# Sine matrices from the sine table instead of from the cosine matrices, and the output bias and row sums moved to other places on TensorE

## The chip, the cores and the metric

The kernel runs on one core of one Trainium2 chip. A core has five engines that run side by side and wait for each other through semaphores: TensorE (PE in the profile; PEld is its weight load), VectorE (DVE), ScalarE (ACT), GpSimd (POOL) and SyncE (SP), which here only starts transfers. Each engine works through its own list of instructions in order: an instruction that waits holds up everything behind it on that engine. The metric is the device time of one execution in microseconds (us). Before the change it is 1546.71 us, the median of three runs that lie between 1543.02 and 1546.88 us.

## The reference, cut to what matters

The program is a forward and backward pass of one block with two mixers: a spectral filter A and a two-layer perceptron B, each behind a modulated layer norm.

```python
def _A_ref(x, w_r, w_i):                      # spectral mixer
    X = jnp.fft.rfft2(x.astype(jnp.float32), axes=(-2, -1))
    X = X * (w_r + 1j * w_i)
    return jnp.fft.irfft2(X, s=(S, D), axes=(-2, -1)).astype(jnp.bfloat16)

def _B_ref(x, w1, b1, w2, b2):                # perceptron, F = 3584
    y = _layernorm(x, axis=-1)
    h = _gelu(jnp.einsum('bsd,df->bsf', y, w1) + b1)
    return jnp.einsum('bsf,fd->bsd', h, w2) + b2

sa, ca, ga, sb, cb, gb = (mod[:, k] for k in range(6))   # mod = silu(c) @ w_mod
h = _layernorm(x) * (1 + ca) + sa
x = x + ga * _A_ref(h, A_w_r, A_w_i)
h = _layernorm(x) * (1 + cb) + sb
x = x + gb * _B_ref(h, B_w1, B_b1, B_w2, B_b2)           # this is out
# reference(): out and the gradients of x, w_r, w_i, w1, b1, w2, b2, c, w_mod for grad_out
```

x is 2048 tokens by 1024 features. The gradient of gb is a sum over the tokens of grad_out times B's output; that output is needed with its bias b2.

## The kernel before: the parts that the change touches

The Fourier transforms are matrix products with cosine and sine matrices, which the kernel makes itself at its start. An index is worked out on GpSimd (`pts`, line 353), reduced modulo the period on VectorE (line 380), and sent through the Sin function of ScalarE (line 381). `gidx` has two halves that are used in turn. Only the cosine matrices CE and CO are made in this way; the sine matrices SE and SO come out of them by `turn`, a GpSimd multiplication of the reversed matrix by a sign for each partition.

```python
genv = reg.tile([P, 3136 + 3 * P], BF16, name="genv", tag="px2")   # index vectors, small rows for b1 and b2
...
def turn(dst, mat):
    pts(dst, mat, sgn[:], None, ALU.mult)                          # GpSimd

def trig(dst, colv, rowv, nrow, width, modn):
    idx = gidx[:, gcount[0] % 2, :]
    gcount[0] += 1
    sh = float(3 * modn // 4)
    for r in range(nrow):
        pts(idx[:, r*width:(r+1)*width], colv, rowv[:, r:r+1], sh, ALU.mult, ALU.add)      # GpSimd, L353
    n = nrow * width
    nc.vector.tensor_scalar(out=idx[:, 0:n], in0=idx[:, 0:n], scalar1=modn - 1, ..., op0=ALU.bitwise_and)  # L380
    nc.scalar.activation(out=dst, in_=..., func=ACT.Sin, bias=negpi[:], scale=2 * np.pi / modn)            # L381
...
# gen_mats: see the diff.  After it, on GpSimd:
nc.gpsimd.dma_start(out=out_7..., in_=gb2r)                        # gradient of b2, L649; gb2r lies in genv
```

The tile `ws2` of the spectral stage has the tag px2 as well, so its loads on SP's queue (L479) can only start when everything that reads `genv` is done. Behind them on the same queue stand the loads of `wt` (L281), transposed pieces of w2 for the first matrix product of the perceptron's gradient (`ph_part`, `pp`, L669). `ph_part` is spread over the spectral stage, to keep TensorE at work while VectorE folds, unfolds and normalizes.

```python
def load_w2t(fg):                                                  # L281, two buffers
    nc.sync.dma_start_transpose(out=wt[:, fg % 2], in_=B_w2[fg * 256:(fg + 1) * 256, :])
for fc in range(PH_EARLY):                                         # PH_EARLY = 6
    ph_part(fc, (0, 1, 2, 3))                                      # 32 matmuls each
    if fc % 2 == 1:
        load_w2t(fc // 2 + 2)
```

The perceptron's forward pass runs in four blocks of 512 tokens. `z_block` (32 matmuls `pz`, then the gelu and its derivative) alternates with seven pieces of `bo_pass` (16 matmuls `pbo` each), once for each block b and half h of the features. TensorE's order is fixed in this stage by `ordered()`.

```python
def bo_pass(b, h):
    pbs = [(ps_f if b < NB - 1 or h == 0 else (ps_s, ps_d)[k % 2])("pbo") for k in range(4)]   # PSUM
    for g in range(7):
        nc.sync.dma_start(out=wp, in_=w2_v[:, g*4:(g+1)*4, cs_])                               # L819
        for i in range(4):
            for k in range(4):
                with ordered():
                    ... matmul(pbs[i][:], lhsT=hh[:, k, i*P:(i+1)*P], rhs=wp[:, k, :],
                               start=(g == 0 and k == 0), stop=(g == 6 and k == 3))             # L824
        if g < 6:
            yield
    ...                                                            # x1t and go (grad_out) are loaded
    for i in range(4):
        last_ev[0] = nc.scalar.copy(out=bo[:, i, :], in_=pbs[i][:])                             # L833
    tt(bo, bo, bcn(b2_row[:, cs_], 4), ALU.add)                    # bias b2, VectorE
    tt(go, go, bo, ALU.mult)
    tt(bo, bo, bcn(gb_row[:, cs_], 4), ALU.mult)
    tt(bo, bo, x1t, ALU.add)
    store_tok_half(out_0, bo, b, h)
    yield
    pa = (ps_s if b == NB-1 and h == 1 else ps_d if b < NB-1 else ps_f)("pa")
    for i in range(4):
        with ordered():
            ... matmul(pa[:], lhsT=ones_bf[:], rhs=go[:, i, :], ...)                            # row sums, L844
    # VectorE adds pa to gacc
...
# in the loop over the plan of the stage; k is the step 0..13 of block b (g here):
    next(boq[b])
    if bo_late and g % 7 == 3:                                     # the row sums of the pass before
        for late in bo_late: next(late, None)
        bo_late.clear()
```

The row sums of the last pass (b=3, h=1) come later, beside the first half of the next product (`pg`, L997), in both kernels; so does the two-pool treatment of the first two w2-gradient rows.

Of the kernel before, what the change touches and what calls it, by code (L numbers as in the profile page):

```python
# [10 lines left out]
FP32 = mybir.dt.float32  # L11
# [24 lines left out]
def kernel(  # L36
# [318 lines left out]
    kevi = iota([[1, 512]], 0, 0, 512)  # L355
    kevc = kevi.bitcast(FP32)
    nc.gpsimd.tensor_copy(out=kevc, in_=kevi)
    kod = gview(512, FP32)
    pts(kod, kevc, 2.0, 1.0, ALU.mult, ALU.add)
    par_i = iota([[1, 1]], 0, 1, 1)  # L360
    nc.vector.tensor_scalar(out=par_i, in0=par_i, scalar1=1, scalar2=None, op0=ALU.bitwise_and)
    sgn = const.tile([P, 1], FP32, name="sgn")
    nc.vector.tensor_scalar(out=sgn[:], in0=par_i, scalar1=-2.0, scalar2=1.0, op0=ALU.mult, op1=ALU.add)
    rown = to_f(iota([[256, 4]], 1, 2, 4), 4)
    rowd = to_f(iota([[256, 2]], 1, 2, 2), 2)
    jf, jod = kevc, kod[:, 0:256]
    gidx = reg.tile([P, 2, 1024], I32, name="gidx", tag="px0")
    gcount = [0]

    def turn(dst, mat):  # L370
        pts(dst, mat, sgn[:], None, ALU.mult)

    def trig(dst, colv, rowv, nrow, width, modn):
        idx = gidx[:, gcount[0] % 2, :]
        gcount[0] += 1
        sh = float(3 * modn // 4)
        for r in range(nrow):
            pts(idx[:, r * width:(r + 1) * width], colv, rowv[:, r:r + 1], sh, ALU.mult, ALU.add)
        n = nrow * width
        nc.vector.tensor_scalar(out=idx[:, 0:n], in0=idx[:, 0:n], scalar1=modn - 1, scalar2=None, op0=ALU.bitwise_and)  # L380
        nc.scalar.activation(out=dst, in_=idx[:, 0:n].rearrange("p (r w) -> p r w", w=width), func=ACT.Sin,  # L381
                             bias=negpi[:], scale=2 * np.pi / modn)
# [3 lines left out]
    em1 = reg.tile([P, 2, 8, 256], BF16, name="em1", tag="px1")  # L386

    def gen_mats():
        for cl, colv, modn in ((CE, kevc, 2048), (CO, kod, 4096)):
            sm = (smA, smB)[cl]  # L390
            for i2 in range(2):
                trig(sm[:, 0, 2 * i2:2 * i2 + 2, :], colv, rown[:, 2 * i2:2 * i2 + 2], 2, 512, modn)
            c0 = 1 - cl
            turn(sm[:, 1, :, c0:512], sm[:, 0, :, 511:0:-1] if c0 else sm[:, 0, :, ::-1])
            if c0:
                turn(sm[:, 1, :, 0:1], sm[:, 0, :, 0:1])
            for k in range(2):
                nc.gpsimd.dma_start(out=d_SF[:, cl + 2 * k], in_=sm[:, k])
        for cl, colv, modn in ((CE, jf[:, 0:256], 1024), (CO, jod, 2048)):
            trig(em1[:, 0, 2 * cl:2 * cl + 2, :], colv, rowd, 2, 256, modn)  # L400
            turn(em1[:, 0, 2 * cl + 4:2 * cl + 6, :], em1[:, 0, 2 * cl:2 * cl + 2, ::-1])
        nc.gpsimd.tensor_scalar(out=em1[:, 1], in0=em1[:, 0], scalar1=2.0 / (S * D), scalar2=None, op0=ALU.mult)
        nc.gpsimd.tensor_scalar(out=em1[:, 1, 0:2, 0:1], in0=em1[:, 0, 0:2, 0:1], scalar1=1.0 / (S * D), scalar2=None, op0=ALU.mult)
        nc.gpsimd.tensor_scalar(out=em1[:, 1, 4:6, 255:256], in0=em1[:, 0, 4:6, 255:256], scalar1=1.0 / (S * D), scalar2=None, op0=ALU.mult)
        nc.gpsimd.dma_start(out=d_E[:], in_=em1[:])
# [348 lines left out]
    n3Ts = [reg.tile([P, NDC, BW], BF16, name="n3Ta", tag="uv3")]  # L754
    otile = []

    b2_row = small.tile([P, D], BF16, name="b2_row", tag="gmrow", bufs=1)

    def after_ph():
        nc.sync.dma_start(out=b2_row[:], in_=B_b2.partition_broadcast(P))  # L760
        t2, t3 = (reg.tile([P, 2, 4, BW], BF16, name=f"gt{k}", tag=f"t{k}") for k in (2, 3))
        gts.append([t2[:, 0], t2[:, 1], t3[:, 0], t3[:, 1], uvp2[:, 0]])
        w2p.append(reg.tile([P, 4, BW], BF16, name="w2sB", tag="ph")[:])
        n3Ts.append(reg.tile([P, NDC, BW], BF16, name="n3Tb", tag="wt"))
        otile.append(reg.tile([P, 3, 4, BW], BF16, name="otile", tag="ot"))
# [47 lines left out]
    def bo_pass(b, h):  # L813
        cs_ = slice(h * KH, (h + 1) * KH)
        pbs = [(ps_f if b < NB - 1 or h == 0 else (ps_s, ps_d)[k % 2])("pbo") for k in range(4)]
        for g in range(7):
            wp = w2p[w2n[0] % 4]
            w2n[0] += 1
            nc.sync.dma_start(out=wp, in_=w2_v[:, g * 4:(g + 1) * 4, cs_])  # L819
            hh = hh_slots[(b * 7 + g) % 11]  # L820
            for i in range(4):
                for k in range(4):
                    with ordered():
                        last_pe[0] = nc.tensor.matmul(pbs[i][:], lhsT=hh[:, k, i * P:(i + 1) * P], rhs=wp[:, k, :],  # L824
                                                      start=(g == 0 and k == 0), stop=(g == 6 and k == 3))
            if g < 6:
                yield
        bo, x1t, go = (otile[0][:, k] for k in range(3))
# [2 lines left out]
        for i in range(4):  # L831
            with tc.high_priority():
                last_ev[0] = nc.scalar.copy(out=bo[:, i, :], in_=pbs[i][:])  # L833
        tt(bo, bo, bcn(b2_row[:, cs_], 4), ALU.add)
        tt(go, go, bo, ALU.mult)
        tt(bo, bo, bcn(gb_row[:, cs_], 4), ALU.mult)
        tt(bo, bo, x1t, ALU.add)
# [31 lines left out]
    for kind, b, g in plan:  # L869
# [7 lines left out]
        else:  # L877
            if g == 0:
                boq[b] = bo_both(b)
            next(boq[b])  # L880
            if bo_late and g % 7 == 3:
                for late in bo_late:
                    next(late, None)
                bo_late.clear()
# [392 lines left out]
```

## Time and profile before

| | |
|---|---|
| time, median of 3 runs | 1546.71 us |
| span of the profiled execution | 1541.1 us |
| PE busy | 1429.6 us (93%) |
| DVE busy | 1083.0 us (70%) |
| ACT busy | 717.7 us (47%) |
| POOL busy | 374.5 us (24%) |
| start, 0 to 130 us: PE busy | 95.43 of 130 us |
| spectral forward stage, 130 to 356 us: PE busy | 216.74 of 226 us |
| seam to the perceptron, 356 to 412 us: PE busy | 50.25 of 56 us |
| perceptron blocks, 412 to 721 us: PE busy | 307.44 of 309 us |
| last block, 721 to 784 us: PE busy | 52.99 of 63 us |
| rest, 784 to 1541 us: PE busy | 706.79 of 757 us |

The lower rows are from a view that gives the busy time of each engine in a stretch of the span. A stretch in which PE is busy throughout gets longer by what is added to PE, and not shorter by what is taken from another engine; in a stretch with gaps on PE, the wait that ends each gap tells what sets the time. Line numbers such as L669 are those of the kernel before.

### The profile page before, as it was taken

The page shows a single profiled execution, that of the slowest core. Times are in us where ns is not written, and L with a number is a line of the kernel's source. Part 1 is how long each engine was busy: PE and PEld are TensorE (multiplying, and loading weights), DVE is VectorE, ACT ScalarE, POOL GpSimd, SP SyncE. Part 2 cuts the span into 40 slices and gives each one's busy share as a digit, 9 for nine tenths or more (in the row PEclk, how much of TensorE's full clock was granted, in tenths as well). Part 3 has the DMA queues.
Part 4 walks back from the last instruction along what each step waited for, and adds up shares of the span by engine and source line. Part 5 has one row for each costly group of instructions (what it writes and reads, how often), then busy time and mean ns, then how long its engine had stood idle before and what let it go on. Part 6 is the DMA issues. An engine that isn't in the chain of part 4 may idle for free.

```text
span 1541.1 us, 18136 instructions
## 1 busy us (share of the span) xinstructions
PE 1429.6 (93%) x6666; PEld 668.8 (43%) x6799; DVE 1083.0 (70%) x1581; ACT 717.7 (47%) x950; POOL 374.5 (24%) x420
## 2 busy tenths in 40 slices
PE   4879899999899999998897999989899889999998
PEld 2434445444344444444343444434344344444443
DVE  5973768897799897887214877959076665898641
ACT  3765555667887666655021323313532345443211
POOL 6710631111112122212111101211133421222422
PEclk7899999999999999999899999999999999999999
DMA  9792654979586776899947336495378876765992
GB/s 336 233 210 74 186 157 143 290 246 348 195 256 237 203 267 239 227 278 266 318 140 234 127 131 218 98 272 151 95 195 222 229 227 178 211 168 164 286 276 94
DMA packets 358302, 324.53 MB, mean 211 GB/s; under 512 B 209202, under 2 KB 300864, under 8 KB 357958
## 3 DMA queue, kind: packets, MB, share of 16 engines
q1 hardware_dynamic: 324326, 207.97, 50.7%
q0 software_dynamic: 33888, 115.41, 21.5%
q8 instruction: 53, 0.87, 0.2%
q14 instruction: 35, 0.29, 0.1%
HBM read 164.41 MB, written 109.10 MB: 177 GB/s over the span
## 4 chain that ended last, share of the span: by engine, by line
PE 33%; DVE 26%; issue 18%; DMA 10%; ACT 6%; POOL 3%; SPq 2%; another core or an unknown queue 0%; POOLq 0%; DVEq 0%; ACTq 0%
PE pbo L824 8%; PE gw2acc L1099 6%; PE pz L786 5%; DVE gt L173 4%; DVE ct L173 3%; PE pv L554 3%; PE pu L461 3%; PE pg L997 2%; PE gw1acc L1177 2%; DVE fbuf L173 2%; ACT ct L451 2%; DVE got L899 1%; DMA xt<-d_gx 1%; DVE x L173 1%; DVE st L427 1%
## 5 line engine op out<-in xcount | busy, mean ns | idle before, releaser
L669 PE MATMUL pp<-gBoT,wt 128*128 128x512 bf16 x876 | 201.3, 383 | 8.8 <-DMA wt<-in_B_w_dram 7.6
L997 PE MATMUL pg<-w1T,gzr 128*128 128x512 bf16 x880 | 196.4, 381 | 1.1 <-ACT gn3a L1010 0.2
L1177 PE MATMUL gw1acc<-gzh,n3n 128*128 128x512 bf16 x877 | 194.6, 379 | 0.8
L669 PEld LDWEIGHTS <-wt 128*128 128x128 bf16 x896 | 88.2, 99 | 114.3 <-DMA wt<-in_B_w_dram 8.1
L786 PEld LDWEIGHTS <-w 128*128 128x128 bf16 x896 | 88.1, 98 | 112.4 <-issue 8.1
L997 PEld LDWEIGHTS <-gzr 128*128 128x128 bf16 x896 | 88.1, 98 | 107.8 <-issue 3.8
L1177 PEld LDWEIGHTS <-n3n 128*128 128x128 bf16 x896 | 87.8, 98 | 103.8
L786 PE MATMUL pz<-n3Ta,w 128*128 128x512 bf16 x438 | 99.8, 383 | 5.8 <-ACT gt L789 5.0
L1099 PE MATMUL gw2acc<-gB,hhsA 128*128 128x512 bf16 x437 | 99.1, 379 | 1.2 <-DMA hhsA<-d_hh 0.7
L786 PE MATMUL pz<-n3Tb,w 128*128 128x512 bf16 x440 | 98.6, 379 | 0.4
L824 PEld LDWEIGHTS <-hhA 128*128 128x128 bf16 x608 | 59.5, 98 | 72.5 <-issue 0.9
L789 ACT ACTIVATE gt<-pz,b_col 128x512 bf16<-128x512 f32 x112 | 73.1, 682 | 29.9 <-PE pz L786 28.5
L795 ACT ACTIVATE gt<-gt 128x2048 bf16<-128x2048 bf16 x28 | 53.5, 1910 | 66.3 <-DVE gt L173 66.2
L1104 ACT CAST gwo<-gw2acc 128x512 bf16<-128x512 f32 x54 | 30.1, 584 | 114.0 <-PE gw2acc L1099 58.2
L173 DVE TENSOR_TENSOR gt<-gt,gt 128x2048 bf16<-128x2048 bf16 x56 | 68.5, 1223 | 20.7 <-ACT gt L797 19.6
L1181 ACT CAST gwo<-gw1acc 128x512 bf16<-128x512 f32 x48 | 27.9, 583 | 110.1 <-PE gw1acc L1177 104.8
L173 DVE TENSOR_TENSOR ct<-ct 128x2048 bf16<-128x2048 bf16 x64 | 75.7, 1217 | 1.6 <-ACT ct L622 0.6
L1099 PEld LDWEIGHTS <-hhsA 128*128 128x128 bf16 x448 | 43.7, 98 | 51.4 <-DMA hhsA<-d_hh 1.2
L1099 PE MATMUL gw2acc<-gB,hht 128*128 128x512 bf16 x250 | 57.3, 386 | 7.3 <-DMA hht<-d_hh 3.9
L791 ACT ACTIVATE gt<-gt 128x2048 bf16<-128x2048 bf16 x28 | 53.5, 1910 | 5.1 <-DVE gb_acc L806 4.4
L797 ACT ACTIVATE gt<-gt 128x2048 bf16<-128x2048 bf16 x28 | 53.4, 1907 | 0.5
L160 POOL DMA_INDIRECT out_dram<-otile,xu x16 | 21.9, 1372 | 126.0 <-DMA out_dram<-otile 25.9
(318 smaller groups left out, 2572.6 us busy)
## 6 DMA issues: line engine op xcount, KB each, us to landing
gzr<-d_gz SPq DMA_DIRECT2D x28, 512.0 KB
wblk<-in_w_mod_dram SPq DMA_DIRECT2D x12, 1024.0 KB
d_ph<-pho POOLq DMA_DIRECT2D x21, 512.0 KB
out_dram<-otl POOLq DMA_DIRECT2D x40, 256.0 KB
d_hh<-hhA POOLq DMA_DIRECT2D x19, 512.0 KB
w2sD<-in_B_w_dram SPq DMA_DIRECT2D x14, 512.0 KB
hhC<-d_ph SPq DMA_DIRECT2D x14, 512.0 KB
w2sA<-d_ph SPq DMA_DIRECT2D x14, 512.0 KB
```

Source lines behind the costliest of these rows:

```text
L173: return nc.vector.tensor_tensor(out=out, in0=a, in1=b, op=op)
L461: last_pu[0] = nc.tensor.matmul(pu[:], lhsT=fb[:, i, cl, c8 * P:(c8 + 1) * P], rhs=sm[:, i, :], start=(i == 0), stop=(i == 3))
L669: last_pe[0] = nc.tensor.matmul(pp[:], lhsT=wt[:, fg % 2, cch, k * P:(k + 1) * P], rhs=gBoT[j][:, cch, :], start=(cch == 0), stop=(cch == ...
L786: last_pe[0] = nc.tensor.matmul(pz[:], lhsT=w1s[g][:, cch, k * P:(k + 1) * P], rhs=n3T[:, cch, :], start=(cch == 0), stop=(cch == NDC - 1))
L789: nc.scalar.activation(out=zb[:, k, :], in_=pz[:], func=ACT.Identity, bias=b1_col[:, fc:fc + 1], scale=1.0)
L791: nc.scalar.activation(out=av, in_=zb, func=ACT.Square)
L795: nc.scalar.activation(out=sg, in_=bv, func=ACT.Sigmoid, scale=2.0 * GK)
L797: nc.scalar.activation(out=bv, in_=bv, func=ACT.Sigmoid, scale=-2.0 * GK)
L824: last_pe[0] = nc.tensor.matmul(pbs[i][:], lhsT=hh[:, k, i * P:(i + 1) * P], rhs=wp[:, k, :], start=(g == 0 and k == 0), stop=(g == 6 and ...
L997: nc.tensor.matmul(pgs[i][:], lhsT=gzt[g][:, k, i * P:(i + 1) * P], rhs=w1Ts[g][:, k, h * KH:(h + 1) * KH], start=(g == 0 and k == 0), sto ...
L1099: nc.tensor.matmul(acc[:], lhsT=hh_s[hh_o[fc]][:, t, :], rhs=gBs[t // 4][:, t % 4, h * KH:(h + 1) * KH], start=(t == 0), stop=(t == NT - 1))
L1177: nc.tensor.matmul(acc[:], lhsT=n3ns[t // 4][:, t % 4, cch * P:(cch + 1) * P], rhs=gz2[t // 8][:, t % 8, :], start=(t == 0), stop=(t == NT ...
```

## The change

Three things change.

First, SE and SO are made as CE and CO are: index on GpSimd, modulus on VectorE, Sin on ScalarE, with another shift. `turn` and its sign column go. This costs six more passes through the chain of three engines, and one more copy and one small fill on GpSimd, and takes away the GpSimd multiplications over whole matrices.

Second, the bias b2 is added by TensorE. Each pass starts with four matmuls with one row of ones as weights and the row b2 as data, which write the bias into the four PSUM tiles; the products then add to it. The VectorE addition over 128 by 2048 elements goes, once for each pass, and b2 is loaded as one row and not copied to 128 partitions.

Third, the row sums of a pass stand two steps earlier in TensorE's order: after the second piece of the next pass and not after the fourth.

```diff
@@ -355,25 +355,21 @@
     kevi = iota([[1, 512]], 0, 0, 512)
     kevc = kevi.bitcast(FP32)
     nc.gpsimd.tensor_copy(out=kevc, in_=kevi)
+    kev = gview(512, FP32)
+    nc.gpsimd.tensor_copy(out=kev, in_=kevc)
+    nc.gpsimd.memset(kev[:, 0:1], 512.0)
     kod = gview(512, FP32)
     pts(kod, kevc, 2.0, 1.0, ALU.mult, ALU.add)
-    par_i = iota([[1, 1]], 0, 1, 1)
-    nc.vector.tensor_scalar(out=par_i, in0=par_i, scalar1=1, scalar2=None, op0=ALU.bitwise_and)
-    sgn = const.tile([P, 1], FP32, name="sgn")
-    nc.vector.tensor_scalar(out=sgn[:], in0=par_i, scalar1=-2.0, scalar2=1.0, op0=ALU.mult, op1=ALU.add)
     rown = to_f(iota([[256, 4]], 1, 2, 4), 4)
     rowd = to_f(iota([[256, 2]], 1, 2, 2), 2)
     jf, jod = kevc, kod[:, 0:256]
     gidx = reg.tile([P, 2, 1024], I32, name="gidx", tag="px0")
     gcount = [0]
 
-    def turn(dst, mat):
-        pts(dst, mat, sgn[:], None, ALU.mult)
-
-    def trig(dst, colv, rowv, nrow, width, modn):
+    def trig(dst, colv, rowv, nrow, width, modn, cosine):
         idx = gidx[:, gcount[0] % 2, :]
         gcount[0] += 1
-        sh = float(3 * modn // 4)
+        sh = float(3 * modn // 4 if cosine else modn // 2)
         for r in range(nrow):
             pts(idx[:, r * width:(r + 1) * width], colv, rowv[:, r:r + 1], sh, ALU.mult, ALU.add)
         n = nrow * width
@@ -386,19 +382,13 @@
     em1 = reg.tile([P, 2, 8, 256], BF16, name="em1", tag="px1")
 
     def gen_mats():
-        for cl, colv, modn in ((CE, kevc, 2048), (CO, kod, 4096)):
-            sm = (smA, smB)[cl]
+        for cl, colv, modn in ((CE, kevc, 2048), (SE, kev, 2048), (CO, kod, 4096), (SO, kod, 4096)):
+            sm = (smA, smB)[cl % 2]
             for i2 in range(2):
-                trig(sm[:, 0, 2 * i2:2 * i2 + 2, :], colv, rown[:, 2 * i2:2 * i2 + 2], 2, 512, modn)
-            c0 = 1 - cl
-            turn(sm[:, 1, :, c0:512], sm[:, 0, :, 511:0:-1] if c0 else sm[:, 0, :, ::-1])
-            if c0:
-                turn(sm[:, 1, :, 0:1], sm[:, 0, :, 0:1])
-            for k in range(2):
-                nc.gpsimd.dma_start(out=d_SF[:, cl + 2 * k], in_=sm[:, k])
-        for cl, colv, modn in ((CE, jf[:, 0:256], 1024), (CO, jod, 2048)):
-            trig(em1[:, 0, 2 * cl:2 * cl + 2, :], colv, rowd, 2, 256, modn)
-            turn(em1[:, 0, 2 * cl + 4:2 * cl + 6, :], em1[:, 0, 2 * cl:2 * cl + 2, ::-1])
+                trig(sm[:, cl // 2, 2 * i2:2 * i2 + 2, :], colv, rown[:, 2 * i2:2 * i2 + 2], 2, 512, modn, cl < 2)
+            nc.gpsimd.dma_start(out=d_SF[:, cl], in_=sm[:, cl // 2])
+        for cl, colv, modn in ((CE, jf[:, 0:256], 1024), (SE, jf[:, 1:257], 1024), (CO, jod, 2048), (SO, jod, 2048)):
+            trig(em1[:, 0, 2 * cl:2 * cl + 2, :], colv, rowd, 2, 256, modn, cl < 2)
         nc.gpsimd.tensor_scalar(out=em1[:, 1], in0=em1[:, 0], scalar1=2.0 / (S * D), scalar2=None, op0=ALU.mult)
         nc.gpsimd.tensor_scalar(out=em1[:, 1, 0:2, 0:1], in0=em1[:, 0, 0:2, 0:1], scalar1=1.0 / (S * D), scalar2=None, op0=ALU.mult)
         nc.gpsimd.tensor_scalar(out=em1[:, 1, 4:6, 255:256], in0=em1[:, 0, 4:6, 255:256], scalar1=1.0 / (S * D), scalar2=None, op0=ALU.mult)
@@ -754,10 +744,10 @@
     n3Ts = [reg.tile([P, NDC, BW], BF16, name="n3Ta", tag="uv3")]
     otile = []
 
-    b2_row = small.tile([P, D], BF16, name="b2_row", tag="gmrow", bufs=1)
+    b2_row = small.tile([1, D], BF16, name="b2_row", tag="gmrow", bufs=1)
 
     def after_ph():
-        nc.sync.dma_start(out=b2_row[:], in_=B_b2.partition_broadcast(P))
+        nc.sync.dma_start(out=b2_row[:], in_=B_b2.rearrange("(o n) -> o n", o=1))
         t2, t3 = (reg.tile([P, 2, 4, BW], BF16, name=f"gt{k}", tag=f"t{k}") for k in (2, 3))
         gts.append([t2[:, 0], t2[:, 1], t3[:, 0], t3[:, 1], uvp2[:, 0]])
         w2p.append(reg.tile([P, 4, BW], BF16, name="w2sB", tag="ph")[:])
@@ -813,6 +803,9 @@
     def bo_pass(b, h):
         cs_ = slice(h * KH, (h + 1) * KH)
         pbs = [(ps_f if b < NB - 1 or h == 0 else (ps_s, ps_d)[k % 2])("pbo") for k in range(4)]
+        for i in range(4):
+            with ordered():
+                last_pe[0] = nc.tensor.matmul(pbs[i][:], lhsT=ones_bf[0:1, :], rhs=b2_row[0:1, cs_], start=True, stop=False)
         for g in range(7):
             wp = w2p[w2n[0] % 4]
             w2n[0] += 1
@@ -822,7 +815,7 @@
                 for k in range(4):
                     with ordered():
                         last_pe[0] = nc.tensor.matmul(pbs[i][:], lhsT=hh[:, k, i * P:(i + 1) * P], rhs=wp[:, k, :],
-                                                      start=(g == 0 and k == 0), stop=(g == 6 and k == 3))
+                                                      start=False, stop=(g == 6 and k == 3))
             if g < 6:
                 yield
         bo, x1t, go = (otile[0][:, k] for k in range(3))
@@ -831,7 +824,6 @@
         for i in range(4):
             with tc.high_priority():
                 last_ev[0] = nc.scalar.copy(out=bo[:, i, :], in_=pbs[i][:])
-        tt(bo, bo, bcn(b2_row[:, cs_], 4), ALU.add)
         tt(go, go, bo, ALU.mult)
         tt(bo, bo, bcn(gb_row[:, cs_], 4), ALU.mult)
         tt(bo, bo, x1t, ALU.add)
@@ -878,7 +870,7 @@
             if g == 0:
                 boq[b] = bo_both(b)
             next(boq[b])
-            if bo_late and g % 7 == 3:
+            if bo_late and g % 7 in (1, 2):
                 for late in bo_late:
                     next(late, None)
                 bo_late.clear()
```

## The prediction

> **What bounds the kernel now.** I read the busy time by stretches first, because one share for the whole span mixes stages with different limits. The columns are: the stretch, its length, then busy time and count for PE, PEld, DVE, ACT and POOL, then the granted clock, the DMA share and GB/s.
>
> ```profile
> 0.00:130.00 130.00, 95.43 (x467) 46.26 (x476) 101.32 (x165) 71.81 (x117) 60.34 (x69) 0.86 0.88 241
> 356.00:412.00 56.00, 50.25 (x222) 22.51 (x226) 36.02 (x61) 46.49 (x48) 6.47 (x9) 0.97 0.83 276
> 412.00:721.00 309.00, 307.44 (x1404) 139.94 (x1431) 269.95 (x403) 209.87 (x192) 69.64 (x71) 1.00 0.83 243
> 721.00:784.00 63.00, 52.99 (x228) 23.22 (x231) 19.25 (x26) 8.35 (x10) 10.01 (x12) 0.92 0.97 309
> ```
>
> The third row is a stretch that TensorE bounds: 307.44 of 309 us. It holds 1404 recorded matmuls, which gives 307.44 / 1404 = 0.219 us; a piece of 16 in mid-stream starts 3.45 us after the one before it, 0.216 us each. I use 0.216. VectorE has 39 us to spare there. The first row is different: TensorE is idle for 34.6 us of 130. So the second view is who waits for whom, for TensorE and for SP's queue in those 130 us (total us, times, longest).
>
> ```profile
> PE pm L233 <- DMA wblk<-in_w_mod_dram: 10.1, 3, 4.3
> PE pt L324 <- DVE gBoT L327: 8.3, 7, 5.3
> PE pp L669 <- DMA wt<-in_B_w_dram: 7.6, 1, 7.6
> SPq L479 <- DMA out_dram<-genv: 12.9, 1, 12.9
> ```
>
> The loads of the first line the change doesn't touch. The second and third lead to code that it touches, and the timeline shows how (start, duration, engine, line).
>
> ```profile
> 27.48 6.17 POOL L353 TENSOR_SCALAR smA<-smA,sgn 128x2044 bf16<-128x2044 bf16 x2
> 28.66 4.81 DVE L380 TENSOR_SCALAR gidx<-gidx 128x1024 int32<-128x1024 int32 x1
> ...
> 65.49 5.41 POOL L402 TENSOR_SCALAR em<-em 128x2048 bf16<-128x2048 bf16 x1
> 70.96 0.56 POOL L649 DMA_DIRECT2D out_dram<-genv  x1
> ...
> 72.72 0.35 SPq L479 DMA_DIRECT2D ws<-in_A_w_r_dram  x1
> 74.54 23.67 SPq L281 DMA_TRANSPOSE wt<-in_B_w_dram  x2
> ...
> 98.35 15.47 PE L669 MATMUL pp<-gBoT,wt 128*128 128x512 bf16 x63 [7.58 <-DMA wt<-in_B_w_dram]
> ```
>
> There are two stories. While GpSimd turns the first sine matrix, VectorE's modulus of the same moment takes 4.81 us, where its sisters take 0.69, and ends about when GpSimd does (33.47 and 33.65 us); the first gBoT of VectorE starts behind it at 33.58, and TensorE waits 5.3 us for that. Later GpSimd, busy with matrices, comes to the small store out of genv only at 70.96; SP's queue stands still until it has landed; behind it are two w2 transposes of 23.67 us, and TensorE waits for them from 90.77 to 98.35.
>
> [...] No matmul of one row and 512 columns is in this trace, so that is an assumption here: 0.216 us for each bias matmul. [...]
>
> **The change, part by part.**
>
> *Bias on TensorE.* Eight passes with four matmuls: 32 x 0.216 = 6.9 us of TensorE. What goes is eight VectorE additions of 1.22 us, 9.8 us, on an engine with time to spare (39 us in the long stretch), so that frees nothing at once. Six passes lie wholly in the stretch that TensorE bounds, and so does the last one (b=3, h=1, from 758 us): they cost 7 x 4 x 0.216 = 6.0 us. The first half of block 3 starts at 721 us, just where TensorE has gaps:
>
> ```profile
> 723.52 1.67 PE L824 MATMUL pbo<-w2sD,hhA 128*128 128x512 bf16 x7 [0.66 <-ACT otile L833]
> 727.22 3.61 PE L824 MATMUL pbo<-w2sB,hhB 128*128 128x512 bf16 x16 [2.02 <-DMA w2sB<-in_B_w_dram]
> 737.56 6.33 PE L824 MATMUL pbo<-w2sA,hhB 128*128 128x512 bf16 x16 [6.73 <-DMA w2sA<-in_B_w_dram]
> ```
>
> Its four matmuls, 0.9 us, and the longer wait for the ACT copies (all four PSUM tiles are asked for at once, not one by one over 2.6 us) fit into the 8.7 us that TensorE waits for w2 pieces anyway. That load stands behind four w1 transposes in SP's queue and doesn't come later. Sum for this part: +6.0 us.
>
> *Row sums two steps earlier.* The work is the same. The question is whether VectorE has go times bo ready. After the pass that ends at 523.89 us, it was multiplied at 531.92 to 533.13, that is 9.2 us later. The new place is one z piece (6.9), two pieces (6.9) and the bias (0.9), 14.7 us after the pass; 5 us in hand, more without the addition. In block 3, where there are no z pieces, the pass that ends at 720.98 has go times bo by 726.6, and the new place can't come before 730.8; for the pass that ends at 758.4 it is 765.4 against 766.2, tight, but 1.2 us come free with the addition. So no new wait; and the row sums of block 2 (4 x 0.216 = 0.9 us, at 747 in the old order) move into the gap of 6.73 us: -0.9.
>
> *Sine matrices.* GpSimd loses 5.45 + 0.73 + 5.45 + two times 2.17 = 16.0 us and gains eight index operations of 0.73, four of 0.76 and a copy of 1.10, 10.0 us; none of the added ones is long. ScalarE gets four Sin of 1.14 and two of 0.71, 6.0 us; VectorE four moduli of 0.69 and two of 0.42, 3.6 us. The instruction order of the changed kernel shows two more things. Before the first product of the spectral stage (pu) VectorE has six more PSUM copies than before, 6 x 0.68 = 4.1 us, which were ScalarE's. And the store out of genv now stands ahead of the 5.41 us scaling and the 3.52 us fill on GpSimd, but behind the last index operation.
>
> Gains: [...] (4.81 - 0.69 = 4.1 us), after which the first gBoT and with it TensorE can start near 29.8 and not 33.6. Then the store out of genv: the chain GpSimd, VectorE, ScalarE for the twelve matrices ends near 60 us, I estimate (after the gBoT copies some six rounds are left, of about 1.5 to 2 us each from 46 us on), so the store is out at 62 and not 71. The first w2 transpose starts when TensorE has given back its buffer, at about 66, not 74.5. The 7.6 us wait goes, and with it 5.64 us that VectorE stood idle at 101 to 107 us for a PSUM tile of that product.
>
> Balance on VectorE, which carries the chain of folds to the first pu at 127.2 us: +3.6 +4.1 -4.1 -5.6 = -2.0 us; another 1.5 us of slow VectorE instructions beside the second turn (47.5 to 52.9) goes too, about -3.5. Against it stand new waits in VectorE's order, where a modulus must wait for GpSimd's index and the Sin before it: I put 1 us. So the spectral stage starts 2.5 us earlier. TensorE alone gains more (up to 10 us of gaps), but it uses this for 25 product matmuls brought forward (the order has 53 where it had 28 ahead of pu), and gains them only as far as VectorE and ScalarE at the seam, 356 to 412 us, keep up: there TensorE waited 5.0 us for ACT. The order of the gelu pieces at the seam changes as well, either way by some us. I count -2.5 for the part.
>
> *Sum:* +6.0 - 0.9 - 2.5 = +2.6 us on 1546.7, 1549.3; I round to 1549.
>
> **The rivals.** *The matrices at the start are worse, not better.* The old way was there to spare ScalarE and VectorE, and at 50 to 80 us VectorE is busy nearly throughout. If VectorE stands at each of the six added moduli for a Sin (1 to 2 us each), the folds come 6 to 9 us later, TensorE runs out of w2 pieces, and the bias comes on top: 1553 to 1560. For it speaks that two index halves are all there are; against it that copies stand between the moduli in the order. *The start gains in full:* if the seam passes on all that TensorE gains (4 us of the gBoT wait, 7.6 of the wt wait, less what new waits take), the start brings 8 to 10 us, and the kernel ends at 1541 to 1544. *The row sums wait.* If the ACT copies of a pass come late, TensorE stands at the new place; at 756 to 763 us two of them did wait 4.3 us for a store. One such wait is 2 to 4 us: 1551 to 1553. *The bias is hidden:* it would be if TensorE were not the bound in the blocks; 1.6 us of gaps in 309 say no.
>
> **Range and chances.** The bias is the firm part: +5 to +7. The start is the open one, -8 to +6. Together 1541 to 1558. Two per cent is 31 us, more than any story here gives: within 2% 0.97, slower 0.02, faster 0.01.
>
> **What would show it.** In the changed profile: 32 bias matmuls with 0.216 us from one start to the next, PE busy some 7 us more in all; from the seam to the end of block 3 about 5 us longer; no VectorE modulus above 1.5 us; the store out of genv near 62, SP's wait for it short, no 7.6 us wait for wt; first pu near 125. No gap ahead of the row sums. It is wrong if the first pu comes later than 127, if the bias matmuls cost clearly less than 0.216 us, or if the gaps at 721 to 743 grow.

## The result and the profile after

The changed kernel takes 1527.64 us (median; 1527.02 to 1531.73) beside 1546.07 us for the kernel before, a ratio of 0.989 with a 95% interval of 0.9868 to 0.9912. Two later measurements beside many more executions of the kernel before gave 0.9907 (0.9874 to 0.9940) and 0.9929 (0.9895 to 0.9963). The kernel before spreads from 1523 to 1551 us in those, with medians of 1537 to 1539 us, so ratios are compared below and not times. The change is worth 11 to 17 us. I had predicted 1549 us and a range of 1541 to 1558. My 1546.7 us for the kernel before lies high in its spread; beside 1538 us the forecast was 2.6 us more, between 6 less and 11 more, and the measured gain lies outside that too.

First the busy times of the changed kernel in the four stretches shown of before (same columns: PE, PEld, DVE, ACT, POOL, clock, DMA share, GB/s).

```profile
0.00:130.00 130.00, 102.24 (x510) 49.34 (x519) 101.65 (x175) 77.80 (x124) 55.70 (x77) 0.92 0.79 243
356.00:412.00 56.00, 55.13 (x251) 24.76 (x255) 43.28 (x69) 46.30 (x46) 9.35 (x12) 1.00 0.79 253
412.00:721.00 309.00, 302.82 (x1367) 135.71 (x1394) 260.64 (x385) 206.12 (x189) 66.06 (x69) 0.99 0.87 246
721.00:784.00 63.00, 59.14 (x260) 26.03 (x265) 14.86 (x23) 8.81 (x12) 9.29 (x11) 0.97 0.87 275
```

TensorE is busier by 6.8 us at the start, by 4.9 at the seam and by 6.2 in the last block, and its clock is nearer to 1 in all three. The stretch that it bounded before holds gaps now (302.82 of 309 us), one of them at the start of block 3, which comes earlier.

The waits of TensorE and of SP's queue in the first 130 us:

```profile
PE pm L233 <- DMA wblk<-in_w_mod_dram: 11.1, 3, 5.4
PE pt L324 <- DVE gBoT L327: 5.5, 8, 2.4
SPq L469 <- DMA out_dram<-genv: 9.7, 1, 9.7
```

The 5.3 us wait behind the modulus of 4.81 us and the 7.6 us wait for wt are gone; of the 8.3 us that TensorE waited for gBoT in all, 5.5 us are left. SP still stands 9.7 us for the genv store, which was 12.9; the two w2 transposes behind this wait in its queue start at 68.90 us and not at 74.54. The timeline shows why the first of these went, and that the store is as early as I had worked out (62 us):

```profile
28.76 0.69 DVE L376 TENSOR_SCALAR gidx<-gidx 128x1024 int32<-128x1024 int32 x1 [1.05 <-POOL gidx L353]
...
62.31 0.57 POOL L639 DMA_DIRECT2D out_dram<-genv  x1
```

The modulus takes 0.69 us, between index operations of GpSimd (27.24 to 28.72 us and from 29.66 us on), where before it took 4.81 us beside two multiplications of 6.17 us. That these held it up was read from the two ends, 33.47 and 33.65 us; no run tests it by itself.

In the last block, TensorE's timeline no longer has the gap of 6.73 us:

```profile
713.27 0.60 PE L808 MATMUL pbo<-b_row,ones_bf 1*128 1x512 bf16 x2
715.73 0.86 PE L808 MATMUL pbo<-b_row,ones_bf 1*128 1x512 bf16 x2 [1.86 <-ACT otile L826]
716.52 5.31 PE L817 MATMUL pbo<-w2sD,hhA 128*128 128x512 bf16 x16
...
726.92 3.61 PE L817 MATMUL pbo<-w2sA,hhB 128*128 128x512 bf16 x16 [0.77 <-DMA w2sA<-in_B_w_dram]
```

The wait for w2sA is 0.77 us; in all, TensorE waits 3.3 us for w2 pieces in this block, where it was 8.7. The wait for the ScalarE copies is 1.86 us and not 0.66, because the bias asks for all four PSUM tiles at once. The sixteen matmuls behind it take 5.31 us in place of 3.6: the granted clock is 0.50 from 717.34 to 720.75 us, as in two of three traces of the changed kernel. More on that below.

### The profile page after: what moved, and what is told of

Read it like the earlier page. It is cut to its first block, busy times and chain, and to the rows that moved or that the text cites. A ratio compares the mean times of both kernels' runs of the same rounds, so it can differ in the third digit from the quotient of the medians.

```text
span 1525.2 us, 18213 instructions
## 1 busy us (share of the span) xinstructions
PE 1432.9 (94%) x6697; PEld 669.0 (44%) x6831; DVE 1072.6 (70%) x1577; ACT 721.6 (47%) x956; POOL 366.1 (24%) x428
## 4 chain that ended last, share of the span: by engine, by line
PE 49%; DVE 18%; issue 14%; DMA 9%; ACT 6%; POOL 3%; SPq 1%; POOLq 0%; ACTq 0%; DVEq 0%
PE pbo L817 11%; PE gw1acc L1169 10%; PE pz L776 9%; PE gw2acc L1091 6%; DVE ct L173 3%; PE pv L544 3%; PE pu L451 3%; PE pg L989 2%; PE pp L659 2%; DVE fbuf L173 1%; DVE got L891 1%; PE po L609 1%; DVE gt L173 1%; DVE x L173 1%; DVE gn3b L896 1%
## 5 line engine op out<-in xcount | busy, mean ns | idle before, releaser
L1174 POOL DMA_DIRECT2D out_dram<-gwo x56 | 30.5, 547 | 80.9 <-ACT gwo L1173 40.1
```

## Stage by stage

I took the start times of TensorE's weight loads, of which nearly none are missing, and cut each kernel's trace at the same five places of its program. The stages are A, to the 33rd matmul pu; B, to the first z; C, blocks 0 to 2, to the first product pbo of block 3; D, block 3, to the first pg; E, to the first gw2acc; F, the rest. Each row is one execution, in us; the ratios come from timed runs. The executions in the rows "TensorE's load only" and "VectorE's relief only" took 9 and 5 us more than the medians of these kernels.

| kernel | A | B | C | D | E | F | ratio to before (95%) |
|---|---|---|---|---|---|---|---|
| before | 133.5 | 223.1 | 364.1 | 63.7 | 227.8 | 528.8 | 1 |
| row sums alone | 128.2 | 224.0 | 365.2 | 61.9 | 227.5 | 530.8 | 1.0010 (0.9990 to 1.0029) |
| bias alone | 126.0 | 223.9 | 376.2 | 55.1 | 223.5 | 534.1 | 1.0006 (0.9985 to 1.0027) |
| bias, row sums | 129.6 | 224.6 | 373.6 | 55.3 | 225.3 | 523.4 | 1.0000 (0.9972 to 1.0029) |
| genv store alone | 128.3 | 215.0 | 365.7 | 61.4 | 226.9 | 529.5 | 0.9946 (0.9915 to 0.9976) |
| genv store, bias | 126.0 | 214.6 | 370.3 | 55.7 | 223.4 | 529.4 | 0.9921 (0.9895 to 0.9946) |
| sine alone | 129.7 | 217.8 | 365.5 | 60.4 | 227.8 | 533.3 | 0.9976 (0.9961 to 0.9991) |
| sine, row sums | 128.7 | 217.3 | 363.7 | 68.3 | 226.2 | 531.8 | 0.9977 (0.9952 to 1.0002) |
| ... with TensorE's load only | 130.2 | 219.3 | 376.1 | 60.9 | 226.5 | 528.4 | 0.9972 (0.9954 to 0.9990) |
| ... with VectorE's relief only | 128.3 | 219.1 | 364.3 | 59.5 | 225.5 | 538.9 | 0.9957 (0.9938 to 0.9976) |
| sine, bias | 128.9 | 217.9 | 370.2 | 54.5 | 223.9 | 524.8 | 0.9923 (0.9896 to 0.9951) |
| changed | 129.7 | 216.7 | 370.2 | 58.8 | 224.1 | 525.7 | 0.9890 (0.9868 to 0.9912) |
| changed, again | 129.1 | 217.6 | 369.8 | 56.0 | 224.9 | 530.2 | 0.9907 (0.9874 to 0.9940) |
| changed, a third time | 129.0 | 217.7 | 370.1 | 55.8 | 224.0 | 526.9 | 0.9929 (0.9895 to 0.9963) |
| changed, VectorE loaded | 128.0 | 217.6 | 374.8 | 54.8 | 225.4 | 530.0 | 0.9989 (0.9972 to 1.0005) |
| changed, full-height bias | 129.1 | 217.8 | 369.0 | 58.4 | 224.6 | 523.8 | 0.9932 (0.9908 to 0.9955) |

The border between C and D stands behind the bias group of block 3. There the four bias matmuls and the wait for the copies within them take 3.25 us in the changed kernel (713.27 to 716.52 above); they count in C, and the kernels without bias matmuls have nothing of the kind there. Where C and D are compared below, I take that into account.

B, C and E repeat within 1 to 2 us among kernels that are alike in them. A, D and F vary more from execution to execution: the four kernels with the old matrices have the same code in A, and 126.0 to 133.5 us. The profile that I predicted from was the slowest of the four there. Its 7.6 us wait for wt is 3.3 us in the profile of the kernel with the row sums alone:

```profile
PE pp L669 <- DMA wt<-in_B_w_dram: 3.3, 1, 3.3
```

With the bias alone it isn't there at all, with bias and row sums it is 6.4 us.

## The experiments

**The parts alone.** Each is the kernel before with one part of the change: the `gen_mats` hunks, the bias hunks, or the line of the row sums.

```diff
+        for cl, colv, modn in ((CE, kevc, 2048), (SE, kev, 2048), (CO, kod, 4096), (SO, kod, 4096)):   # sine
+                last_pe[0] = nc.tensor.matmul(pbs[i][:], lhsT=ones_bf[0:1, :], rhs=b2_row[0:1, cs_], ...)  # bias
+            if bo_late and g % 7 in (1, 2):                                                                # sums
```

> The kernel before with the sine matrices of the changed kernel alone (bias and row sums as before). Theory: these matrices bring the whole gain and the seam passes it on; in the changed kernel's trace the first z matmul comes 10.3 us earlier and the hidden layer's middle of block 0 (440 us) 14.5 us earlier, so I expect 14 to 21 us less than before, 1525 to 1532 us, with the first z near 346.5 us. Rival, the prediction's own term: VectorE's folds carry the start and only 2.5 us come through, about 1543.5 us, first z near 354; then the gain of the changed kernel comes from the bias or the row sums.

> The kernel before with the bias on TensorE alone. Theory: six passes in the stretch that TensorE bounds pay 4 x 0.216 us each, and in the changed kernel's trace the lead does shrink by 6.7 us between 440 and 714 us; what follows may give back the 4.4 us that the changed kernel gained between 721 and 784 us if these are the bias's doing (output rows ready 1.22 us sooner). So 1548 to 1552 us if the bias only costs, 1546 to 1548 us if it also brings the 4.4 us. Rival (the bias is hidden or even helps by taking an addition off VectorE): at or below 1545 us.

> The kernel before with the row sums taken two steps earlier alone; the instruction order differs from before only where the sums move. Theory: no new wait, 0.9 us of work moved into the gap near 740 us, 1545 to 1546 us. Rival 1: the earlier place waits for VectorE's product go times bo, 2 to 4 us a time, 1548 us or more. Rival 2: the readout of the sums was what held the w2 piece and with it the gap of 6.7 us near 737 us in block 3, since the buffer behind that piece also holds the sums; then 1541 to 1543 us and that gap is shorter.

Measured: 0.9976, 1.0006 and 1.0010. On 1538 us that is -3.7, +0.9 and +1.5 us, the last two not to be told from nothing. So the sine matrices alone don't bring the whole: they gain 6 us in B as the theory said (first z at 347.4), but the time falls by 3.7 us only. The bias alone costs 11 to 12 us in C (376.2 beside 364 to 365; 3.2 of it is the group of block 3) and gets it back in D and E. The row sums do nothing, neither the wait of the first rival nor the gain of the second.

> The changed kernel with the bias back on VectorE (sine matrices and row sums changed). Theory: the bias is a pure cost of 6 to 7 us on TensorE, so this is faster than the changed kernel by that: 1520 to 1523 us. Rival: the bias on TensorE pays for itself by freeing VectorE at the end of each pass, so without it the time is the same or longer, 1527 to 1531 us.

Measured: 0.9977, slower than the changed kernel by 0.5 to 0.9 per cent. This is where my theory fell: taking the bias off TensorE should have saved 6 us, and it cost 7 to 13.

**The whole, beside the parts.**

> The changed kernel as it is, beside the kernel before on the same chip, with many runs of both; the first comparison had four of each, all of before at 1543 to 1547 us, while 67 later runs of before spread from 1528 to 1548 us with a median of 1538. Theory (parts add): the parts alone gave -3.7 us (sine matrices), +0.9 (bias), +1.5 (row sums), so the whole gives -1 to -4 us on a before of 1538, a ratio of 0.997 to 0.999. Rival (the whole is worth more than its parts, as the first ratio says): 0.989, 1521 us.

Measured: 0.9907. The rival holds: the whole is worth more than its parts.

> The changed kernel with the row sums back at their old place (sine matrices and bias changed). Theory (the row sums are only moved work, the bias pays with the sine matrices): 0.990 to 0.993, as the changed kernel. Rival (the early sums are what lets the bias pay, since the reading out of the sums then comes earlier and releases the buffer it shares with a w2 piece): 0.996 to 0.999.

> The changed kernel with the sine matrices made the old way (bias and row sums changed). Theory (bias and sine matrices need each other): 0.999 to 1.002. Rival (bias and row sums need each other, the sine matrices just add their 0.002): 0.992 to 0.995.

> The changed kernel once more, beside the others on this chip: 0.989 to 0.993 if the first two measurements hold (0.989 and 0.991); 0.996 or above if they were favourable.

Measured: 0.9923, 1.0000 and 0.9929. Without the row sums the gain is the same, and without the sine matrices it isn't there. It takes the sine matrices and the bias together.

**What of the bias pays.** It puts four matmuls on TensorE and takes an addition from VectorE. Four kernels separate the two. The first two leave the changed sine matrices and row sums and either keep VectorE's addition and put four matmuls of 128 rows, later overwritten, on TensorE, or leave the bias out (the output lacks it). The third is the changed kernel with an addition of another row put back on VectorE (the output holds it). The fourth does the bias with full-height matmuls.

```diff
+  matmul(pbs[i][:], lhsT=ones_bf[:], rhs=gb_row[:, cs_], start=True, stop=True)      # TensorE's load only
-  tt(bo, bo, bcn(b2_row[:, cs_], 4), ALU.add)                                        # VectorE's relief only
+  tt(bo, bo, bcn(gb_row[:, cs_], 4), ALU.add)                                        # changed, VectorE loaded
+  matmul(pbs[i][:], lhsT=ones_bf[:], rhs=b2_row[:, cs_], ...)                        # changed, full-height bias
+  # b2_row: 128 rows, zero but for the first
```

> Sine matrices and row sums changed, the bias added by VectorE as before, but four matmuls of 128 rows and 512 columns, whose result is overwritten, stand on TensorE where the changed kernel has its bias matmuls: TensorE's delay and its waits for PSUM without VectorE's relief. Beside it: the changed kernel 0.991 of before, the same kernel without these matmuls 0.998. Theory A (delay: TensorE comes later to the w2 pieces of block 3, which DMA times, so the gaps and the half-clock stretches behind them go): 0.990 to 0.993. Theory B (VectorE's relief is what pays): no gain and 6.9 us more on TensorE, 1.000 to 1.003.

> Sine matrices and row sums changed, and the bias left out altogether (the first output lacks it): VectorE's relief without TensorE's 6.9 us. Theory A (delay): the gaps of block 3 stay, 0.996 to 0.998. Theory B (VectorE's relief): the changed kernel's 0.991 less 6.9 us, 0.985 to 0.988.

> The changed kernel with one addition of 128 x 2048 per pass put back on VectorE at its old place (of another row, so the first output is wrong by it), the bias on TensorE as well: only VectorE's relief is taken back. Theory V (relief pays: the changed chain of VectorE sends the stores and with them SP's loads off earlier): 0.996 to 1.000. Theory D (TensorE's delay or the order of instructions pays): as the changed kernel, 0.990 to 0.993.

> The changed kernel with the bias matmuls of full height (128 rows of ones against a tile that holds the bias in its first row and zeros below), the addition gone from VectorE. Theory V (the addition off VectorE pays): as the changed kernel, 0.990 to 0.993, the bias matmuls 0.216 us apart. Rival (one-row matmuls are what pays, or the order that comes with them): 0.996 to 0.999, as with full-height matmuls and the addition left on VectorE.

Measured: 0.9972, 0.9957, 0.9989 and 0.9932. Putting the addition back takes away all of the gain (0.9989), and full-height matmuls without the addition keep it (0.9932), with it don't (0.9972): VectorE's relief is needed. But alone it gives 0.9957, and not the 0.985 to 0.988 of theory B. So TensorE's load seems to help too, but that is not shown: the intervals touch those of the changed kernel, and in its trace C, D and E sum to 649.3 us, no more than the 649.9 to 653.1 of the changed kernel. Neither theory holds as it was put.

The traces show one place for each. TensorE's timeline in the kernel with VectorE loaded, and VectorE's of the same time:

```profile
525.48 1.03 PE L837 MATMUL pa<-otile,ones_bf 128*128 128x512 bf16 x4
526.34 5.34 PE L776 MATMUL pz<-n3Ta,w 128*128 128x512 bf16 x24
534.95 3.43 PE L776 MATMUL pz<-n3Ta,w 128*128 128x512 bf16 x8 [3.26 <-DVE w2sD L840]
```

```profile
533.09 1.22 DVE L173 TENSOR_TENSOR hhA<-gt,gt 128x2048 bf16<-128x2048 bf16 x1
534.22 0.67 DVE L840 COPY w2sD<-pa 1x512 f32<-1x512 f32 x1
```

And the changed kernel (third execution), TensorE and VectorE:

```profile
527.16 1.03 PE L836 MATMUL pa<-otile,ones_bf 128*128 128x512 bf16 x4
528.02 7.09 PE L776 MATMUL pz<-n3Ta,w 128*128 128x512 bf16 x32
```

```profile
532.50 0.67 DVE L839 COPY w2sD<-pa 1x512 f32<-1x512 f32 x1
```

The row sums pa and every other z tile share one PSUM pool of two tiles. The next z matmul can't start before VectorE has read pa. TensorE has finished pa at 526.5 us, but VectorE's queue holds eight microseconds of other work, and comes to the reading at 534.22. TensorE stands for 3.26 us there, and then does eight matmuls in 3.43 us and not 1.9 (the granted clock is 0.89 on average from 530 to 545 us), together 4.8 us; in the changed kernel it doesn't stand at all (32 matmuls in one run). C is 374.8 beside 370.0 us: all of the difference in C. By the ratios the addition costs 9 us; the rest has no place yet. Half of the wait comes from VectorE, whose reading is 1.7 us later than in the changed kernel, and half from TensorE, which is done with pa 1.7 us earlier. VectorE's order is another one too: in the kernel with VectorE loaded the product hhA stands ahead of the reading, in the changed kernel behind it.

One rule fits this place in all the kernels of the table: TensorE waits by as much as the reading comes more than 4.4 us after the end of pa (4.3 us in the changed kernel, no wait; 6.6 with the sine matrices alone, 2.15 us; 7.7 with VectorE loaded, 3.26 us). That is the time of the 24 z matmuls less the reading itself. The additions are one thing that sets the delay, and not the only one: the wait is 3.4 us with TensorE's load only, 3.1 us with the bias alone and 2.9 us where the bias is left out, and the kernel before, with all its additions, has none (4.5 us).

The other place is block 3. Waits of TensorE in it, first for sine matrices with row sums (no bias on TensorE), then for the kernel with VectorE loaded:

```profile
PE pbo L814 <- DMA w2sA<-in_B_w_dram: 4.7, 1, 4.7
PE pbo L814 <- DMA w2sB<-in_B_w_dram: 4.5, 1, 4.5
PE pbo L814 <- DMA w2sD<-in_B_w_dram: 1.5, 1, 1.5
```

```profile
PE pbo L808 <- ACT otile L826: 1.9, 1, 1.9
PE pbo L817 <- DMA w2sA<-in_B_w_dram: 0.2, 1, 0.2
```

With the bias on TensorE, D is 54.5 to 58.8 us in all the kernels of the table, without it 59.5 to 68.3, and E is 223.4 to 225.4 beside 225.5 to 227.8. In D half of the difference is the border: with the group of block 3 counted in, it is 57.7 to 62.1 us, on average 3 us less than without, and the ranges overlap. I took the rest for delay (TensorE comes later to w2 pieces that SP's queue sends at its own time), but with TensorE's load only D is 60.9 us, and 64.2 with its group. What goes with it is how long the 28 w1 transposes take, which stand ahead of those pieces in SP's queue: 53 to 62 us in total in the table's kernels with the bias on TensorE, 62 to 79 us in those without. Why they do is open; VectorE's relief isn't the cause, since the kernel with VectorE loaded has 57 us.

**Do delays vanish in block 3?** The bias matmul three times (the output holds three times the bias), and the w1 transposes put behind the w2 loads of block 3:

```diff
+            for r in range(3):
+                matmul(pbs[i][:], lhsT=ones_bf[0:1, :], rhs=b2_row[0:1, cs_], start=(r == 0), stop=False)
```

```diff
+    W1T_AFTER = [(2, 1, 6), (3, 0, 0), (3, 0, 2), (3, 0, 4), (3, 1, 0), (3, 1, 2), (3, 1, 4)]
+            with tc.issue_after(w2_ld[W1T_AFTER[g]].ins):
                 nc.sync.dma_start_transpose(out=wtile[:, k, :], ...)
```

> The changed kernel with each bias matmul done three times into the same sum (64 more matmuls; the output then holds three times the bias). That is 64 x 0.216 = 13.8 us more on TensorE. Theory (DMA gates): block 3's w2 pieces and the first rows of the input gradient come at times that SP's queue sets, and TensorE stands 4 to 10 us at each of them, so a delay ahead of them is mostly hidden: 3 to 8 us more than the changed kernel. Rival (TensorE is the bound throughout, as the prediction has it): 12 to 14 us more.

> The changed kernel with the w1 transposes of block 3 spread out in SP's queue so that the w2 pieces of block 3 come ahead of them (the same loads, another order). Theory (DMA gates): the waits for w2 pieces between 705 and 784 us, 3.3 us in the changed kernel and 4 to 11 us in the others, shrink to under 1 us and the kernel gains 2 to 5 us on the changed one, unless the transposes then come late for the first input-gradient pass. Rival (these waits are bandwidth of the chip's DMA engines, 0.92 to 0.99 busy there, not order): same as the changed kernel within 1 us, with the waits moved to the first input-gradient pass.

Measured: 1.0078 and 1.0011. The first is 26 us more than the changed kernel, nearly twice the 13.8 us of its matmuls: no gate hides it, and the rival was too low as well. The second is 16 us more; the waits for w2 pieces grew to 10.3 us in D (67.2 us). Spreading the transposes over 687 to 776 us puts one ahead of nearly every w2 piece; before they began at 622. The order that I thought better was worse.

TensorE's timeline in the kernel with three bias matmuls says where most of the other half came from:

```profile
567.05 7.07 PE L776 MATMUL pz<-n3Ta,w 128*128 128x512 bf16 x32
574.05 2.76 PE L809 MATMUL pbo<-b_row,ones_bf 1*128 1x512 bf16 x12
576.74 5.31 PE L818 MATMUL pbo<-w2sC,hhA 128*128 128x512 bf16 x16
581.89 3.62 PE L818 MATMUL pbo<-w2sD,hhA 128*128 128x512 bf16 x16
```

There is no gap, and yet the sixteen matmuls behind the twelve one-row ones run at half clock: 5.31 us and not 3.62, with a granted clock of 0.89 on average from 575 to 590 us. It happens behind five of the eight groups, once with a wait of 1 us within the group (the expectation below says six; five is right). Five times 1.7 us is 8.5 us.

> The changed kernel with two matmuls of 128 rows, whose result is overwritten, ahead of each bias matmul: as many more matmuls (64, 13.8 us) as the kernel with the bias done three times, but these of full height. There each group of twelve one-row matmuls in a row was followed by 3.4 us of TensorE at half clock (6 of 8 passes seen), and it took 26 us more than the changed kernel. Theory [...]: no half-clock stretch behind these groups, 10 to 16 us more than the changed kernel, a ratio of 0.998 to 1.001 to before. Rival (the half clock comes from the delay or the order, not from the rows): 22 us or more, 1.005 and above.

The edit puts two full-height matmuls, later overwritten, ahead of each one-row bias matmul. Measured: 1.0059, some 23 us more than the changed kernel, by its number the rival. But the trace has no half clock behind any of these groups, and the mean clock of the execution is 0.982, where it is 0.976 with three one-row matmuls:

```profile
575.67 0.38 PE L811 MATMUL pbo<-b_row,ones_bf 1*128 1x512 bf16 x1
575.98 3.63 PE L820 MATMUL pbo<-w2sC,hhA 128*128 128x512 bf16 x16
```

So the half clock goes here with the few rows, and not with the delay, and the time went elsewhere: a group of twelve that alternates between heights takes 3.41 us (572.57 to 575.98) and not 2.6, eight times 0.8 us. With 13.8 us that is 20 of the 23.

**An earlier start in another way.** The small store out of genv and the small load into it issued from ScalarE's queue: in the kernel before, in the changed kernel, and in the kernel before with the bias.

```diff
-    nc.gpsimd.dma_start(out=out_7..., in_=gb2r)
-    nc.gpsimd.dma_start(out=b1r, in_=B_b1...)
+    nc.scalar.dma_start(out=out_7..., in_=gb2r)
+    nc.scalar.dma_start(out=b1r, in_=B_b1...)
```

> The kernel before with only the small store out of genv and the small load into it issued from ScalarE's queue instead of GpSimd's, so that they no longer stand behind the matrices. The order of TensorE's work stays nearly that of before (28 product matmuls ahead of the first spectral product). Theory: the wait for w2 at 91 to 98 us goes but the work of TensorE between the first pu and the first z stays, since what the sine matrices gain is the 25 product matmuls that the new order puts into TensorE's early gaps; so -0 to -2 us, first z at 350 to 353 us. Rival (the release of genv is the gain): -3.5 us and the first z at 346 to 347 us.

> The changed kernel with the small genv store and load issued from ScalarE's queue, the edit that alone took 8 us from the kernel before. Theory (both shorten the same start: the sine matrices gain by releasing genv and w2 earlier): little on top, 0.988 to 0.991. Rival (they add): 0.985 to 0.986.

> The kernel before with the genv store and load issued from ScalarE's queue (0.995 alone) and the bias on TensorE (1.001 alone), the sine matrices made the old way, the row sums at their old place. Theory (the bias pays wherever VectorE then reads the row sums out in time, which an earlier start decides): below 0.991, that is 1526 us or less. Rival (the bias pays only in the company of the sine matrices' order): 0.995 to 0.998.

Measured: 0.9946, 1.0003 and 0.9921. The first refutes my theory: B gets 8 us shorter. It doesn't separate the release of genv from the order, though: the new order has 20 more product matmuls ahead of the 33rd pu (it was to stay as before), where that of the sine matrices has 26 more. On the changed kernel the same edit is harmful: the order of the start is another one, and A takes 136.6 us. The third gives the bias an earlier start without the sine matrices, and it pays against the store alone: with the group of block 3 counted in D, C is 1.4 us longer, D 2.5 and E 3.5 us shorter, and TensorE's longest wait for the reading of pa is 0.8 us and not 2.2. It didn't get below 0.991, but the sine matrices as such aren't what the bias needs.

No version is clearly faster than the changed kernel; those with sine matrices and bias, and the last one, are level with it.

## Why the prediction was wrong

**The step that failed** is the bias. I wrote of the VectorE additions that they went "on an engine with time to spare (39 us in the long stretch), so that frees nothing at once", and put "+6.0 us" into the sum. Added to the sine matrices the bias brings 0.9976 to 0.9923, about -8 us. The cost itself was sized nearly right: a group of four takes 0.96 us and not 0.86, so six passes cost 5.8 us and not 5.2. What I left out is that TensorE waits for VectorE and ScalarE in C, the stretch that I called bound by TensorE, and that the bias changes these waits. Take the four executions with sine matrices and bias on TensorE beside the two with sine matrices and the addition on VectorE, the group of block 3 counted in D. C is only 2.2 us longer on average (1.3 and 3.1 beside the one and the other), though six groups cost 5.8. TensorE's waits for VectorE and ScalarE in C are 6.4 us with the sine matrices alone and 5.7 with sine matrices and row sums, and 2.8 to 3.4 us in the four. With the sine matrices alone eight matmuls at half clock, 1.6 us more, stand behind one of these waits:

```profile
548.36 3.49 PE L776 MATMUL pz<-n3Ta,w 128*128 128x512 bf16 x8 [2.15 <-DVE w2sD L837]
```

The shorter waits and the slow matmuls that are gone make up what C wins back. So the 39 us of VectorE's idleness are an average: at 526 to 534 us, with the addition put back, it had none, and TensorE was waiting for it. D is 4.8 us shorter and E 2.8; the cause there is open, and the 4.8 are rough (60.4 and 68.3 us in the two without). F is 5.6 us shorter, but in it single executions differ by more, so I can't say that the bias does that. None of my rivals had a gain from the bias.

**The sine matrices** were -2.5 us in my sum and -3.7 (-6.0 to -1.4) alone: right in size, wrong in where. A of the changed kernel is no shorter than that of the four executions of the old start (129.3 us on average both); my 2.5 us were read from an execution that had an unlucky start. B is 6.6 us shorter in the changed kernel, since 26 product matmuls, 5.6 us, moved into TensorE's gaps. I had named them and doubted that the seam would pass them on. It does: TensorE's waits for ScalarE fell from 5.0 to 1.9 us there. The rival "the start gains in full" had the right mechanism, and its 8 to 10 us are what the first z shows (346.5 beside 353 us on average, 6 to 7); less than that is left at the end without the bias.

**The row sums**: -0.9 predicted, +1.5 (-1.5 to +4.5) alone and no difference within the whole. No gap ahead of them, right. The wait stands behind them, for the reading of pa, which I didn't look for.

**What would show it:** moduli of 0.70 us at most, genv store at 62, no wait for wt: right. SP's wait short: no, 9.7. First pu near 125: I had misread the trace. The pu at 127.24 us is the seventh, and six stand ahead of it from 118.84 on; the seventh comes at 123.60 in the changed kernel, the first at 109.92.

```profile
118.84 0.81 PE L461 MATMUL pu<-smA,fbuf 128*128 128x512 bf16 x3
127.24 0.60 PE L461 MATMUL pu<-smA,fbuf 128*128 128x512 bf16 x2 [0.69 <-DVE fbuf L173]
```

```profile
123.60 0.60 PE L451 MATMUL pu<-smA,fbuf 128*128 128x512 bf16 x2 [0.35 <-DVE fbuf L173]
```

From the seam to the end of block 3, 5 us longer: only 1.1 in the first pair of traces (first z to first pg). The gaps at 721 to 743 us: I expected them to hide the bias of one pass; they shrank.

**Half clock.** I saw the sixteen matmuls of 6.33 us behind the long gap and didn't count such places. The clock records of the traces hold two values, 1.00 and 0.50, in pieces of 3.41 us. Half clock lasts 91.4 us in the trace before (61.3, 68.3 and 75.4 in the others with the old start, 74 on average) and 60.3, 44.8 and 51.1 us in the three of the changed kernel, 52 on average. Matmuls run in 54.5 of the 74 us and in 42.1 of the 52. The sixteen matmuls of 5.31 us lost 1.7 us in a piece of 3.41 us, half of it; by that, some 6 us of the gain may be such stretches that went with their gaps; that is an estimate from averages whose single values touch (61.3 and 60.3). In the trace before, the clock is 0.50 from 732.86 to 743.10 us, around the end of the gap of 6.73 us at 737.56. What sets off half clock is not shown, and the length of a single gap doesn't tell: the gap of 2.02 us ahead of 727.22 had none (1.00 from 720 to 730 us), single gaps of 2.06 us with three bias matmuls and of 2.15 us with the sine matrices alone had a piece.

## What to carry to other kernels

Idle time of an engine in a stretch doesn't say that its work is free: look for the moment at which another engine waits for one instruction in its queue, and count what stands ahead of it. A stage border in such a table should stand where the kernels are alike. Price a gap on TensorE at its length and, where a piece of half clock can follow, at half of that piece more (1.7 us here). One execution's waits for transfers vary by several us, and a small edit can reorder a whole start: measure parts together with their partners before adding them up.

## What the runs showed of the hardware that I had not expected

- At the second z behind a row sum, gaps of TensorE of 2.06 to 3.26 us came with a piece of half clock in all six kernels that had them (2.15 us with the sine matrices alone, then 3.41 us at 0.50, with eight matmuls in 3.49 us), and one of 3.42 us, with TensorE's load only, came with none, the eight matmuls taking 1.89 us:

```profile
538.80 1.89 PE L776 MATMUL pz<-n3Ta,w 128*128 128x512 bf16 x8 [3.42 <-DVE w2sD L841]
```

- Twelve one-row matmuls in a row, 2.7 us of work, were followed by half clock five times of eight (sixteen matmuls in 5.31 us); with two full-height ones ahead of each, in eight groups, never (3.63 us).
- A one-row matmul costs more where the height changes: one-row groups of four 0.96 us, full-height ones 0.86, alternating twelve 3.41 and not 2.6.
- The same 28 transposes took 53 to 79 us in SP's queue in the kernels of the table.
